# One snapshot of the fifth output product instead of two, and another order of the output products

## The chip, the cores and the metric

The kernel runs on one core of one Trainium2 chip. The metric is the time of one execution in device microseconds, as the median of several runs. Engines are named as the profile names them: PE (TensorE matmul), PEld (TensorE weight load), DVE (VectorE), ACT (ScalarE), POOL (GpSimd), SP (SyncE, which here only issues transfers).

## The reference, cut to what matters

Attention over 8 batches, 8 heads, 576 positions and a head size of 64, then a bilinear feed-forward layer:

```python
rel = pos[:, None] - pos[None, :]
mask_local = (rel >= 0) & (rel < 32)                                   # heads 0 to 3
mask_strided = (rel >= 0) & (pos[None, :] % 32 == pos[:, None] % 32)   # heads 4 to 7
scores = np.where(mask, scale * q @ k.T, -1e9)
attn = softmax(scores) @ v                        # (8, 8, 576, 64)
x = attn.transpose(0, 2, 1, 3).reshape(4608, 512)
out = ((x @ w_a) * (x @ w_b)) @ w_out             # d_ff = 1536, out (4608, 512)
```

Both masks keep so few positions that the kernel works on small groups of them (96 or 72 queries against 128 or 72 keys) and not on the whole square.

## The kernel before

**Tiles and slots.** The 4,608 tokens are nine tiles `t` of 512. A tile has sixteen slots: twelve slots `ffn_ab` (line 581: the products of `x` with a block of `w_a` and of `w_b`, eight matmuls of 512 columns; ACT copies the first, line 598; DVE multiplies it with the second into `pf`, line 601), then four slots of the output product. The attention of batch t+1 runs in the slots of tile t, so that its results `xT` are there for the next tile. The order on every engine is the order of the program: nothing is rescheduled, and each engine works its queue from the front.

**Attention steps.** Each batch has eight steps `S0` to `S7` and eight steps `V0` to `V7`, two for each pair of heads. An `S` step is a group of small matmuls into the PSUM tile `st` (line 384), an exponential by ACT (line 392) and a mask by DVE (line 402). A `V` step is a group of six or eight small matmuls into the PSUM tile `o` (line 485), a logarithm and an exponential by ACT (lines 494 and 495, which make the reciprocal of the row sums) and two multiplications by DVE into `xT` (lines 499 and 501). There is one `st` and, from the second tile on, one `o`, so a `V` step can begin on PE only when the two multiplications of the `V` step before it have read `o`. The dictionary `LATER` gives the slots of these steps; `IN_Y` gives the last three, which lie between products of the output stage.

**Output stage of tiles 2 to 7.** `y_plan` works the product with `w_out` by a scheme of Strassen's kind. Halves of `pf` and sums of halves (`ps`, line 615, by DVE) meet halves of `w_out` and sums of halves (`wf`) in seven products, named "1" to "7". Each is made for two halves of its rows, q = 0 and 1; in `Y_ORDER` "50" is product 5, q = 0. One such half is six matmuls of 256 columns (line 669). Three PSUM tiles collect them, each of exactly one bank, with q = 0 in its first half and q = 1 in its second: X takes products 1, 6, 5 and 3 one after the other on top of each other, Z takes 7 and then 4, Y takes 2. Because X is a running sum, ACT must copy its state out (a "snapshot") before the next product adds to it. `y_post` does that: for 1, 7, 6 and 5 an ACT copy (line 646), for 3 an ACT copy (line 652), for 4 and 2 an addition by DVE (lines 648 and 650), and "+" adds 7's copy to 5's snapshot (DVE, line 644). All are done for both halves together when q = 1 is complete; only product 5 is copied half by half, 128x256 after "50" and 128x256 after "51". A call `take(("y", t, n))` behind the n-th entry of `Y_ORDER` runs the attention step that `IN_Y` has at n. When all is done, two transfers from SP store the tile (line 664), in slots 2 and 3 of the next tile.

**Last tile.** `y_tail` works the same products for tile 8, in `TAIL_ORDER`, with a bank of its own for each half (in the trace `mm` and, for q = 1, `end`; matmuls at line 700). It has no attention beside it and stores each quarter as soon as it is complete: through SP after "+" of 50 and of 51 and after 20, through ACT's queue after 31, and after 21, whose columns are cut in two, once through ACT and once through SP (line 635).

**Pacing of loads.** POOL issues the loads of later batches. Before those of a slot, it copies one element of that slot's result (`pace`, line 908), so that the loads do not run ahead. In the third of the four output slots the element lies in the part of `y` that holds product 5's snapshot.

Of the kernel before, what the change touches and what calls it, by code (L numbers as in the profile page):

```python
# [30 lines left out]
def kernel(  # L31
# [139 lines left out]
    def fast_w(n, gs):  # L171
        a, b = ((wov[:, 0, 1], wov[:, 0, 0]), (wov[:, 1, 1], wf[:, 0]), (wov[:, 1, 1], wov[:, 0, 1]),
                (wov[:, 1, 0], wf[:, 1]))[n]
        nc.vector.tensor_tensor(wf[:, n, gs], a[:, gs], b[:, gs], op=ALU.subtract)
# [349 lines left out]
    def step_X(b, c):  # L524
# [19 lines left out]
                 27.5: "V4", 28: "S6", 28.5: "V5", 29: "S7", 29.5: "V6", 30.5: "V7"}}  # L544
    LATER = {-1: "S0", 0: "S1", 1: "V0", 2: "S2", 3: "V1", 4: "S3", 5: "V2", 6: "S4", 7: "V3", 8: "S5", 9: "V4", 10: "S6",
             11: "V5"}
    IN_Y = {3: "S7", 5: "V6", 11: "V7"}
    FN = {"Tk": step_Tk, "Tq": step_Tq, "S": step_S, "V": step_V, "X": step_X, "W": lambda b, n: fast_w(n, slice(0, 3)),
          "s": S_px, "m": S_m, "L": lead_vl, "Pk": lambda b, c: pair_up("k", c), "Pq": lambda b, c: pair_up("q", c),
          "Z": lambda b, n: zero_qz(0, nc.vector, ((1, 1),)), "D": lambda b, n: step_D(FIRST_D, 0, "k", n)}  # L550
# [8 lines left out]
    def take(pos):  # L559
        for b, names in steps.get(pos, ()):  # L560
            run(b, names)
# [5 lines left out]
    def mm_bank(shape):  # L567
        nm = "tp" if used[0] % 4 == 3 and used[0] >= 0 else "mm"
        used[0] += 1
        return psum4[nm].tile(shape, F32, tag=nm, name="mm")  # L570
# [49 lines left out]
    def products(t):  # L620
        pf, s = pfs[t], pss[t]
        full = lambda e, i: (lambda g, q: pf[:, 2 * g + e, HT * i + q:HT * (i + 1):2])
        summed = lambda n: (lambda g, q: s[:, n, g, q:HT:2])
        wsum = lambda n: (lambda g: wf[:, n, g])
        wfull = lambda e, j: (lambda g: wov[:, e, j, g])
        return {"1": ("X", full(0, 0), wfull(0, 0)), "2": ("Y", full(1, 0), wfull(1, 0)), "3": ("X", summed(3), wfull(1, 1)),
                "4": ("Z", full(1, 1), wsum(3)), "5": ("X", summed(0), wsum(0)), "6": ("X", summed(1), wsum(1)),
                "7": ("Z", summed(2), wsum(2))}
# [8 lines left out]
    def y_bufs():  # L637
        return [fsb.tile([128, 2, d_model], F32, tag="y_sb", name="y_sb", bufs=2) for _ in range(2)]

    def y_post(k, y, q, bank, n=slice(0, HN)):  # L640

        part = lambda i, j: y[i][:, q, HN * j:HN * (j + 1)]
        if k == "+":
            nc.vector.tensor_tensor(part(1, 1), part(1, 1), part(0, 1), op=ALU.add)
        elif k in "1765":
            nc.scalar.copy({"1": part(0, 0), "7": part(0, 1), "6": part(1, 0), "5": part(1, 1)}[k], bank)  # L646
        elif k == "4":
            nc.vector.tensor_tensor(part(1, 0), bank, part(1, 0), op=ALU.add)
        elif k == "2":
            nc.vector.tensor_tensor(y[0][:, q, n], bank, y[0][:, q, n], op=ALU.add)  # L650
        elif k == "3":
            nc.scalar.copy(part(0, 1), bank)

    Y_ORDER = [(x[0], int(x[1])) for x in "10 11 70 71 20 60 61 40 41 50 51 21 30 31".split()]
    TAIL_ORDER = [(x[0], int(x[1])) for x in "10 70 11 71 60 61 40 41 50 51 30 20 31 21".split()]

    def y_plan(t):

        plan, y = products(t), y_bufs()
        bank = {x: mm_bank([128, 2, HN]) for x in "ZXY"}  # L660

        def store_half(i):
            rows = out[TTOK * t:TTOK * (t + 1)].rearrange("(a i s q) c -> a s i (q c)", i=2, s=8, q=2)
            nc.sync.dma_start(out=rows[:, :, i], in_=y[i].rearrange("p q c -> p (q c)"))

        for n, (k, q) in enumerate(Y_ORDER):
            b, lhs, rhs = plan[k]
            for g in range(FG):
                nc.tensor.matmul(bank[b][:, q], lhsT=lhs(g, q), rhs=rhs(g), start=k in "172" and q == 0 and g == 0,  # L669
                                 stop=g == FG - 1, skip_group_check=True)  # L670
                if g == FG - 1:
                    if k == "5":
                        y_post(k, y, q, bank[b][:, q])
                    elif q == 1:
                        y_post(k, y, slice(0, 2), bank[b])
                    if (k, q) == ("5", 1):
                        y_post("+", y, slice(0, 2), None)
                    take(("y", t, n + 1))
                yield y
        do(16 * t + 18, store_half, 0)  # L680
        do(16 * t + 19, store_half, 1)

    def y_tail(t):
# [4 lines left out]
                  "Z": pst.tile([128, 2, 512], F32, tag="st", name="end")[:, 0, :HN]}]  # L688
        for k, q in TAIL_ORDER:
            b, lhs, rhs = plan[k]  # L690
# [25 lines left out]
    def ffn_ys(t, j, mid):  # L716
        if j == 0:
            yst[t] = (y_tail if t == NT - 1 else y_plan)(t)
        for i in range(21):
            y = next(yst[t])  # L720
            if i == 10:
                mid()
        if j == 3:
            for _ in yst[t]:
                pass
        return (y[0][:1, 0, :1], None, y[1][:1, 0, HN:HN + 1], y[1][:1, 0, :1])[j]
# [36 lines left out]
    with tc.manual_schedule(engines={ENG.PE, ENG.SP, ENG.Pool, ENG.DVE, ENG.Activation}):  # L763
# [76 lines left out]
        for b in range(1, B):  # L840
            for pos, names in (STEPS.get(b) or {16 * (b - 1) + x: n for x, n in LATER.items()}).items():
                steps.setdefault(pos, []).append((b, names.split()))
            if b not in STEPS:
                for n, names in IN_Y.items():
                    steps["y", b - 1, n] = [(b, names.split())]
# [3 lines left out]
        def do(i, fn, *args):  # L849
            at.setdefault(i, []).append(lambda: fn(*args))  # L850
# [91 lines left out]
```

## Time and profile before

| | before |
|---|---|
| median of 3 runs | 334.27 us (333.74 to 334.72) |
| profiled execution, its time | 333.48 us |
| profiled execution, its span | 331.7 us |
| PE, PEld busy | 320.4 us (97%), 205.2 us (62%) |
| DVE, ACT, POOL busy | 252.6 (76%), 211.3 (64%), 151.0 us (46%) |
| granted TensorE clock | 1.00 |
| span of one middle tile (93 to 128 us) | 35.0 us |
| output stage in it (116.10 to 127.04 us) | 10.94 us |

A row of the timeline has the start, the duration and the engine of an instruction or of several alike, then line, operation, the tile written and those read, and in brackets how long the engine had been idle and what released it. Matmuls are pipelined: the next starts before the last has drained, so the time that PE gives to a group is read from start to start and not from the durations.

### The profile page before, as it was taken

Reading aid. Unit: us, or ns where it says so; the run is one execution under the profiler, and the core shown is the slowest. Engines: PE = TensorE matmul, PEld = TensorE weight load, DVE = VectorE, ACT = ScalarE, POOL = GpSimd, SP = SyncE. Lnnn points to the kernel's source line nnn. Section 1 sums busy time; section 2 is a strip of 40 time slices with the busy share of each in tenths; the row PEclk is TensorE's granted clock in tenths of the full one; section 3 lists DMA queues with packets and bytes.
Section 4 is the critical chain, followed back from the end, with each engine's and each line's share of the span. In section 5 each row is a group of like instructions: output and inputs, shape, how many; then the busy total and the mean of one; then the engine's idle time right before and its main releaser. Section 6 shows DMA issues by size and latency. Waiting matters only on the chain.

```text
span 331.7 us, 7639 instructions
## 1 busy us (share of the span) xinstructions
PE 320.4 (97%) x2788; PEld 205.2 (62%) x2820; DVE 252.6 (76%) x529; ACT 211.3 (64%) x351; POOL 151.0 (46%) x280
## 2 busy tenths in 40 slices
PE   8999999999999999999999999999999999999994
PEld 6754655455555576557899875567555854574474
DVE  7766978889778997899879977997878655626652
ACT  6764775487788766887577767876777643333341
POOL 8936838699866355654366455543011001100000
PEclk9999999999999999999999999999999999999999
DMA  9999999999998987999889996998023040004004
GB/s 159 152 205 196 204 178 207 147 172 130 131 208 125 86 90 66 118 207 100 76 83 216 102 103 51 195 135 97 0 73 116 2 129 0 0 3 126 0 2 126
DMA packets 98725, 37.50 MB, mean 113 GB/s; under 512 B 76672, under 2 KB 95744, under 8 KB 98688
## 3 DMA queue, kind: packets, MB, share of 16 engines
q0 software_dynamic: 85968, 19.48, 63.5%
q1 hardware_dynamic: 12432, 17.34, 17.8%
q8 instruction: 22, 0.36, 0.5%
q10 hardware_dynamic: 288, 0.20, 0.2%
q14 instruction: 15, 0.12, 0.1%
HBM read 39.51 MB, written 9.44 MB: 148 GB/s over the span
## 4 chain that ended last, share of the span: by engine, by line
PE 87%; DVE 6%; ACT 3%; issue 2%; DMA 1%; SPq 0%; DVEq 0%
PE mm L581 50%; PE mm L669 14%; PE mm L734 6%; PE st L384 4%; PE o L485 4%; DVE xT L501 2%; PE mm L700 2%; PE o L441 1%; DVE pf L601 1%; DMA raw<-in_q_dram 1%; PE end L700 1%; DVE ps L615 1%; PE ab L581 1%; DVE tq L326 1%; ACT xr L495 1%
## 5 line engine op out<-in xcount | busy, mean ns | idle before, releaser
L581 PE MATMUL mm<-xT,wb_sb 128*128 128x512 bf16 (+1 forms) x465 | 109.1, 357 | 0.2
L581 PE MATMUL mm<-xT,wa_sb 128*128 128x512 bf16 (+1 forms) x451 | 107.7, 356 | 1.1
L598 ACT COPY a_sb<-mm 128x512 f32<-128x512 f32 x106 | 62.0, 585 | 45.3 <-PE mm L581 44.6
L908 POOL CAST pace<-pf 1x1 f32<-1x1 bf16 x87 | 24.5, 281 | 122.6 <-DVE pf L601 120.2
L581 PEld LDWEIGHTS <-wb_sb 128*128 128x128 bf16 x480 | 46.3, 98 | 44.0 <-issue 0.2
L601 DVE TENSOR_TENSOR pf<-a_sb,mm 128x512 bf16<-128x512 f32 x84 | 57.0, 678 | 18.2 <-PE mm L581 14.2
L581 PEld LDWEIGHTS <-wa_sb 128*128 128x128 bf16 x480 | 42.7, 98 | 31.2
L392 ACT ACTIVATE p<-st 128x576 bf16<-128x576 f32 (+1 forms) x64 | 41.6, 650 | 7.6 <-PE st L384 7.0
L494 ACT ACTIVATE xr<-o 64x576 f32<-64x576 f32 x48 | 31.1, 647 | 23.8 <-PE o L485 23.5
L495 ACT ACTIVATE xr<-xr 64x576 f32<-64x576 f32 x48 | 32.8, 683 | 1.5
L669 PEld LDWEIGHTS <-ps 128*128 128x128 bf16 x288 | 27.5, 98 | 6.8 <-issue 3.8
L499 DVE TENSOR_TENSOR xT<-o,xr 64x288 bf16<-64x288 f32 x48 | 21.6, 449 | 13.3 <-ACT xr L495 12.7
L669 PE MATMUL mm<-wf,ps 128*128 128x256 bf16 x216 | 28.3, 272 | 2.8 <-ACT y_sb L646 2.8
L646 ACT COPY y_sb<-mm 128x512 f32<-128x512 f32 (+1 forms) x34 | 16.5, 485 | 20.6 <-PE mm L669 17.3
L501 DVE TENSOR_TENSOR xT<-o,xr 64x288 bf16<-64x288 f32 x48 | 21.6, 449 | 9.9 <-ACT xr L495 9.4
L734 PE MATMUL mm<-wo_sb,pf 128*128 128x512 bf16 x93 | 22.9, 379 | 0.1
L669 PEld LDWEIGHTS <-pf 128*128 128x128 bf16 x216 | 20.6, 98 | 2.7 <-issue 0.2
L242 POOL DMA_DIRECT2D vs<-in_v_dram x24 | 19.6, 818 | 5.0 <-ACT p L392 2.4
L669 PE MATMUL mm<-wo_sb,pf 128*128 128x256 bf16 x144 | 18.7, 272 | 0.1
L211 POOL DMA_DIRECT2D ql<-in_q_dram x24 | 16.0, 665 | 5.6 <-DMA wo_sb<-in_moe_w_out_dram 4.5
L211 POOL DMA_DIRECT2D kl<-in_k_dram x24 | 16.0, 666 | 5.0 <-issue 3.2
L615 DVE TENSOR_TENSOR ps<-pf 128x512 bf16<-128x512 bf16 (+1 forms) x48 | 17.7, 380 | 0.5
(152 smaller groups left out, 468.6 us busy)
## 6 DMA issues: line engine op xcount, KB each, us to landing
out_dram<-y_sb SPq DMA_DIRECT2D x12, 512.0 KB, 4.8
out_dram<-y_sb SPq DMA_DIRECT2D x11, 256.0 KB, 3.0
vl<-in_v_dram POOLq DMA_DIRECT2D x6, 384.0 KB, 6.4
kl<-in_k_dram POOLq DMA_DIRECT2D x24, 72.0 KB, 3.2
ql<-in_q_dram POOLq DMA_DIRECT2D x24, 72.0 KB, 3.7
vs<-in_v_dram POOLq DMA_DIRECT2D x24, 72.0 KB, 3.9
wo_sb<-in_moe_w_out_dram POOLq DMA_DIRECT2D x4, 384.0 KB, 9.6
natk<-in_k_dram POOLq DMA_DIRECT2D x20, 72.0 KB, 3.5
```

The costliest lines, as they stand in the source:

```text
L211: nc.gpsimd.dma_start(out=t[32 * h:32 * h + 32], in_=src[b, h].rearrange("(i y) d -> y i d", y=32))
L392: nc.scalar.activation(p[:M, :, :W], st[:M, :, :W], ACT.Exp, scale=scale)
L494: nc.scalar.activation(r, sums, ACT.Ln)
L495: nc.scalar.activation(r, r, ACT.Exp, scale=-1.0)
L499: nc.vector.tensor_mul(dst[:, W * half:W * (half + 1)], o[:64, j, :W], r[:, j])
L501: nc.vector.tensor_mul(dst.rearrange("d (p r) -> d p r", r=RS)[:, :, G * half:G * (half + 1)], o[:64, j, :W].rearrange("d (g p) -> d p g", ...
L581: nc.tensor.matmul(ps_[:, c0:c0 + n], lhsT=w[:, kk, 128 * f:128 * (f + 1)], rhs=xT[:, kk, x0:x0 + n], start=(kk == first and c0 == 0), sto ...
L598: nc.scalar.copy(a_sb, ab[0])
L601: nc.vector.tensor_mul(pf[:, f, :].rearrange("p (i a s) -> p a i s", i=2, s=16), halves(a_sb), halves(ab[1]))
L669: nc.tensor.matmul(bank[b][:, q], lhsT=lhs(g, q), rhs=rhs(g), start=k in "172" and q == 0 and g == 0, stop=g == FG - 1, skip_group_check=True)
L734: nc.tensor.matmul(ybank[j], lhsT=pf[:, f, 128 * j:128 * (j + 1)], rhs=wo_sb[:, f], start=(f == 0), stop=(f == FD - 1))
L908: nc.gpsimd.tensor_copy(pace, done)
```

## The change

The snapshot of product 5 becomes one copy of 128x512 after "51", as it is for the other products. Product 2 is no longer split: in `Y_ORDER` its first half moves from between 71 and 60 to behind 51, so that 20 and 21 both lie between 51 and 30. `IN_Y` moves with it: S7 from behind the first half of product 7 to ahead of it (behind 11), V6 from behind 20 to behind 61, and V7 stays eleventh, which is now between 20 and 21 where it was between 51 and 21. In the last tile 31 moves ahead of 20, and the stores that hang on 31 and on 20 with them.

```diff
-    IN_Y = {3: "S7", 5: "V6", 11: "V7"}
+    IN_Y = {2: "S7", 6: "V6", 11: "V7"}
...
-    Y_ORDER = [(x[0], int(x[1])) for x in "10 11 70 71 20 60 61 40 41 50 51 21 30 31".split()]
-    TAIL_ORDER = [(x[0], int(x[1])) for x in "10 70 11 71 60 61 40 41 50 51 30 20 31 21".split()]
+    Y_ORDER = [(x[0], int(x[1])) for x in "10 11 70 71 60 61 40 41 50 51 20 21 30 31".split()]
+    TAIL_ORDER = [(x[0], int(x[1])) for x in "10 70 11 71 60 61 40 41 50 51 30 31 20 21".split()]
...
                 if g == FG - 1:
-                    if k == "5":
-                        y_post(k, y, q, bank[b][:, q])
-                    elif q == 1:
+                    if q == 1:
                         y_post(k, y, slice(0, 2), bank[b])
-                    if (k, q) == ("5", 1):
-                        y_post("+", y, slice(0, 2), None)
+                        if k == "5":
+                            y_post("+", y, slice(0, 2), None)
                     take(("y", t, n + 1))
```

The sequences of an output stage, with the attention steps in their places:

| | order on PE |
|---|---|
| before | 10 11 70 S7 71 20 V6 60 61 40 41 50 51 V7 21 30 31 |
| after | 10 11 S7 70 71 60 61 V6 40 41 50 51 20 V7 21 30 31 |

The number of matmuls does not change. ACT has one instruction less in each of six tiles. In DVE's queue "+" moves ahead of one transposition (line 331).

## The prediction

> **What bounds the kernel now.** I read the page first, then PE's waits, then the timeline of one output stage, last a table of all six.
>
> ```profile
> PE 320.4 (97%) x2788; PEld 205.2 (62%) x2820; DVE 252.6 (76%) x529; ACT 211.3 (64%) x351; POOL 151.0 (46%) x280
> L581 PE MATMUL mm<-xT,wb_sb 128*128 128x512 bf16 (+1 forms) x465 | 109.1, 357 | 0.2
> ```
>
> PE bounds it: 97% busy, and the large matmuls of line 581 lost 0.2 us to idling. So only time that PE loses inside the output stages can be won. PE's waits name it:
>
> ```profile
> PE mm L669 <- ACT y_sb L646: 2.8, 6, 0.5
> PE o L485 <- DVE xT L501: 0.6, 3, 0.2
> ```
>
> Six times (once for each of tiles 2 to 7) a product waits for a snapshot; three times a V step waits for DVE. The timeline of tile 2's stage shows the places:
>
> ```profile
> 118.95 0.91 DVE L501 TENSOR_TENSOR xT<-o,xr 64x288 bf16<-64x288 f32 x2
> 118.99 0.82 PE L669 MATMUL mm<-wo_sb,pf 128*128 128x256 bf16 x6
> 120.00 0.42 PE L485 MATMUL o<-p,vs 72*128 72x72 bf16 x8 [0.20 <-DVE xT L501]
> 121.57 1.47 PE L669 MATMUL mm<-wf,pf 128*128 128x256 bf16 x12
> 122.88 0.82 PE L669 MATMUL mm<-wf,ps 128*128 128x256 bf16 x6
> 123.73 0.37 ACT L646 COPY y_sb<-mm 128x256 f32<-128x256 f32 x1 [1.30 <-PE mm L669]
> 124.16 0.81 PE L669 MATMUL mm<-wf,ps 128*128 128x256 bf16 x6 [0.46 <-ACT y_sb L646]
> ```
>
> The row at 122.88 is 50, the copy at 123.73 its half snapshot, the row at 124.16 is 51. They use different halves of bank X, yet 51 starts 0.06 us after the copy's end (124.10). Twelve matmuls (40 and 41) took 122.88 - 121.57 = 1.31 us, 0.109 each, so 51 could have started at 122.88 + 0.66 = 123.54: the loss is 0.62 us, more than the 0.46 of the row, which counts from the modelled end. In the same way 20 (118.99) would have let V6 in at 119.65; V6 came at 120.00, 0.14 us after V5's multiplications, which end at 119.86: 0.35 us lost.
>
> All six stages, from the start of 10 to the first matmul behind 31:
>
> ```profile
> 116.10:127.04 10.94, 10.29 (x115) 8.94 (x112) 9.02 (x19) 7.14 (x12) 6.56 (x13) 1.00 0.76 87
> 151.10:162.03 10.93, 10.28 (x114) 8.94 (x111) 9.01 (x19) 7.14 (x12) 6.57 (x13) 1.00 0.76 85
> 186.59:197.23 10.64, 10.18 (x108) 8.91 (x108) 8.75 (x18) 7.09 (x12) 6.55 (x13) 1.00 0.78 87
> 221.29:232.23 10.94, 10.28 (x114) 8.93 (x111) 9.02 (x19) 7.14 (x12) 4.44 (x9) 1.00 0.69 85
> 256.30:266.88 10.58, 10.12 (x113) 9.00 (x111) 6.58 (x15) 7.14 (x12) 0.25 (x2) 1.00 0.01 2
> 287.60:297.39 9.79, 9.33 (x86) 8.23 (x84) 4.23 (x8) 2.50 (x5) 0.37 (x1) 1.00 0.01 2
> ```
>
> First comes the length. Without a wait a stage takes 84 x 0.1093 = 9.18 us, and in the first five 0.77 more for S7, V6 and V7 (0.26, 0.25, 0.26 from start to start): 9.95. The excess is 0.99, 0.98, 0.69, 0.99, 0.63 and 0.61: 4.89 us in all, 6 x 0.62 = 3.7 of it before 51, the rest before V6 (0.36, 0.35, 0.07, 0.36, 0). The clock was 1.00 in all of them.
>
> **The change, step by step.** Times from here on count from the start of 10 in tile 2, with no wait: 10 at 0, 11 at 0.66, S7 1.32, 70 1.58, 71 2.23, 60 2.89, 61 3.55, V6 4.20, 40 4.45, 41 5.11, 50 5.76, 51 6.42, 20 7.07, V7 7.73, 21 7.98, 30 8.64, 31 9.30, end 9.95. Each must find what it needs; the times of ACT and DVE come from rows of the same timeline, moved with the PE row that releases them.
>
> *One snapshot of product 5.* 51 follows 50 with nothing to wait for: -0.62 us in six stages, -3.7. The wait goes to 30, the next to add to X. A whole copy takes 0.58 (rows of other products) and starts about 0.31 after the last matmul's start (6.97): 7.28 to 7.87. With 0.06 to release, 30 could go at 7.93 and is due at 8.64: 0.71 spare, 0.45 in tile 7, which has no V7. The cover is 20, V7 and 21 (1.57 us); without it the stage would lose about 0.9. ACT works 0.58 instead of 2 x 0.37 us, which PE does not feel.
>
> *Where page and row differ.* The rows at 122.88 to 124.16 show the half copy causing PE's pause. The Trainium skill, Perfetto Trace Analysis, section "Optimizing Scalar/DVE Operations", says that where Scalar or Vector are not saturated but cause bubbles elsewhere, breaking up their instructions may let work finish sooner. ACT is at 64%, so by that rule the halves should stay; merging would cost 0.58 - 0.37 = 0.21 us in six stages, +1.3 us, if 30 stood right behind the copy, and the whole change would come to +0.3 and 334.6 us. I go by the rows.
>
> *V6 behind 61.* V5's multiplications end at 3.76, release at 3.90; V6 is due at 4.20: -1.14 us in all. Its p was masked long before (step S6). Next is V7, which waits for V6's chain, and that now starts with an ACT queue holding 6's snapshot ahead of it: snapshot 4.41 to 5.00, logarithm and exponential (0.65, 0.68) to 6.38, multiplications 6.41 to 7.30 (DVE is free from 5.44). V7 may go at 7.45 and is due at 7.73: 0.28 spare, the smallest margin here.
>
> *S7 ahead of 70.* Its bank `st` was read before the stage began. ACT takes 1's snapshot, S7's exponential and 7's snapshot in the order of before: nothing.
>
> *60 earlier.* It needs 1's snapshot (ended at 2.18, due 2.89) and the last `ps` rows, which DVE finished at 2.92. Those are for its fifth and sixth matmuls, at 3.33: spare 0.4.
>
> *DVE, SP, POOL.* "+" runs at about 8.6 and then one transposition, so V7's multiplications start near 9.9 and end by 10.9; the next tile reads them after S0 and six large matmuls, at 11.46: nothing. The moved steps issue no transfer; SP's order in tiles 2 to 7 stays. The third `pace` now waits for "+" and not for 50's copy, 9.4 instead of 8.1; behind it in POOL's queue stand the loads kl and ql, which landed by 128.7 and are read from 137.8 on: hidden. If they were late, DVE's transpositions would be, and then S0.
>
> *Last tile.*
>
> ```profile
> 324.89 0.37 ACT L646 COPY y_sb<-end 128x256 f32<-128x256 f32 x1 [0.28 <-PE end L700]
> 326.00 0.82 PE L700 MATMUL end<-wo_sb,ps 128*128 128x256 bf16 x6
> 327.19 0.63 DVE L650 TENSOR_TENSOR y_sb<-mm,y_sb 128x128 f32<-128x128 f32 x2 [0.57 <-PE mm L700]
> out_dram<-y_sb SPq DMA_DIRECT2D x3, 256.0 KB, 2.9
> ```
>
> 31 moves from 326.00 to 325.35 and needs 51's copy, over at 325.26 plus 0.06: it just fits. Its 128 KB go out 0.65 us earlier, the 256 KB of 20 by 0.65 later (issue 327.3), and DVE's additions for 21 start 0.1 later, behind that of 20. With 2.9 us to landing the 256 KB arrive at 330.2, about when the last store landed (issued 327.9, 2.6 us). Bounds: -0.2 (ACT's last store freed of the one ahead of it) to +0.4 us (the engines empty 0.4 later). I take +0.1, nearer to the landing row.
>
> *Sum.* -3.74 - 1.14 + 0.1 = -4.8 us. For small losses at margins under 0.4 us I give back 0.1: -4.7. The profiled execution took 333.48 us (span 331.7, the rest lies around it); 333.48 - 4.7 = 328.8; the median lay 0.79 above, so 329.6 us.
>
> **The rivals.**
> *V7 takes over V6's wait.* Margin 0.28 us; if ACT or DVE come 0.3 to 0.6 later than I reckon, five stages lose 0.05 to 0.3. With V6's 1.14 gone entirely: 334.27 - 3.7 = 330.6, range 330.3 to 331.5. For it: V6 did just that. Against it: DVE idled 0.32 us before V6's multiplications, so it isn't late there. 0.22.
> *The faster stage outruns something behind it.* Tile 4's S4 started at 176.04, its last transfer landed at 175.62. DVE is busy for 30.6 of tile 3's 35 us. A loss of 0.3 us in each of five tiles and the V6 part gone: 332.1. Against it: DVE still idles 0.9, 0.8 and 0.4 us early in tile 3's first slots (before rows of line 499), where it catches up. 0.05.
> *It doesn't remove the wait.* If 51 were held by something else of X, only V6's part would come: 333.1, at the edge of no change, and no change if one margin fails as well. Against it: the release 0.06 us after the copy, six times. 0.05.
> *Slower: 5's snapshot comes late.* If ACT gets to it after V7's logarithm and exponential (8.19 to 9.55), it ends at 10.14, and 30 goes at 10.2 instead of 8.64: 1.56 lost in five stages, 7.8 against 4.9 won, 337.2 us. It costs from a start of the copy after 8.0, and turns the sum from 8.85 on. For it: ACT's queue is in order, and such a pair takes 1.36 us. Against it: the copy is queued ahead of V7's pair, and ACT is free from 6.4. 0.06.
>
> **How the numbers follow.** The forecast has 0.62 (328.8 to 330.3: the tail's bounds and the spread of the runs, 0.5 each way); with V7's wait 0.84. The range 328.6 to 331.6 takes in both and leaves some 0.16 out. A measurement can tell about 0.3%, 1.0 us, from no change. Faster: 0.62 + 0.22 + 0.05 = 0.89; same 0.05; slower 0.06.
>
> **What would show it.** Right: PE's waits have no row of line 669 for ACT, 51 starts 0.66 us after 50, the stages take 9.95 and 9.18 us, ACT has six instructions fewer with copies of 0.58 us. Half right: a row "PE o" for DVE xT at V7. Wrong: 30 released by an ACT copy, the first matmuls of the next tile idle, or a stage above 10.6 us.

## The result, and the profile after

The changed kernel took 329.66 us (median of 4 runs, 329.22 to 330.64), beside 334.19 us for the kernel before (333.74 to 334.72): a ratio of 0.9868, 95% interval 0.984 to 0.9896. The prediction was 329.6 us, between 328.6 and 331.6. Some executions, of the kernel before too, ran at a mean granted clock of 0.980 to 0.990 and took some 3 to 6 us longer than the others of their kernel: one of the six of e2 below, three of the six of e9, one of the six of e12.

Line 669 is the output stage in both kernels; below `y_plan` the changed kernel's lines are lower by two. First the busy time and the number of instructions of each engine, then the whole list of PE's waits:

```profile
PE 322.3 (98%) x2820; PEld 206.2 (63%) x2820; DVE 251.6 (76%) x529; ACT 210.2 (64%) x345; POOL 151.4 (46%) x280
```

```profile
PE misc L154 <- PEq L924: 0.9, 1, 0.9
PE o L441 <- DMA tk<-in_v_dram: 0.6, 1, 0.6
PE tp L286 <- ACT shared L798: 0.5, 1, 0.5
PE o L441 <- DMA vl<-in_v_dram: 0.3, 1, 0.3
```

There is no row of line 669 and none of line 485 left; these four belong to the first 20 us, before anything that was changed. ACT has 345 instructions where it had 351. The timeline of PE in tile 2's stage (it starts at 118.09) runs from group to group:

```profile
119.66 2.79 PE L669 MATMUL mm<-wf,ps 128*128 128x256 bf16 x24
122.28 0.43 PE L485 MATMUL o<-p,vs 72*128 72x72 bf16 x8
122.55 1.48 PE L669 MATMUL mm<-wf,pf 128*128 128x256 bf16 x12
123.86 1.47 PE L669 MATMUL mm<-wf,ps 128*128 128x256 bf16 x12
125.17 0.82 PE L669 MATMUL mm<-wo_sb,pf 128*128 128x256 bf16 x6
125.82 0.42 PE L485 MATMUL o<-p,vs 72*128 72x72 bf16 x8
```

The rows are 70 to 61 in one piece, V6, 40 and 41, 50 and 51, 20, and V7. V6 comes 2.62 us after 70 began, which is 24 matmuls at 0.109; 51 follows 50 within one row. No row has a bracket for idle time. In the same stage ACT makes product 5's whole copy, and DVE the two multiplications of V6:

```profile
125.37 0.59 ACT L646 COPY y_sb<-mm 128x512 f32<-128x512 f32 x1 [0.86 <-PE mm L669]
124.54 0.92 DVE L501 TENSOR_TENSOR xT<-o,xr 64x288 bf16<-64x288 f32 x2 [1.01 <-ACT xr L495]
```

The six stages, by stretch (length first, then busy time and number for PE, PEld, DVE, ACT and POOL, then the granted clock and two figures of the DMA engines):

```profile
118.09:128.05 9.96, 9.96 (x114) 9.02 (x111) 8.75 (x19) 6.88 (x11) 4.32 (x9) 1.00 0.68 77
152.12:162.08 9.96, 9.96 (x114) 9.00 (x111) 8.75 (x19) 6.88 (x11) 4.33 (x9) 1.00 0.69 77
186.64:196.60 9.96, 9.96 (x109) 9.00 (x109) 8.50 (x18) 6.83 (x11) 4.32 (x9) 1.00 0.68 76
220.66:230.62 9.96, 9.96 (x114) 9.00 (x111) 8.75 (x19) 6.89 (x11) 4.46 (x9) 1.00 0.72 78
254.69:264.65 9.96, 9.96 (x113) 9.00 (x111) 6.62 (x15) 6.89 (x11) 0.26 (x2) 1.00 0.01 2
285.37:294.54 9.17, 9.17 (x85) 8.22 (x84) 4.34 (x8) 2.34 (x4) 0.37 (x1) 1.00 0.01 2
```

PE is busy for the whole of each. They add up to 58.97 us where they added up to 63.82: 4.85 us. (The end of tile 6's stage in the kernel before, 266.88, is worked out at 0.109 us per matmul: the first matmul behind it has no record in the trace.) The rest of the way from the first stage to the last tile's products, with no output stage in it, took 138.2 us in both kernels.

This profiled execution took 330.64 us, the longest of the four, and its first stage began at 118.09 us where it was 116.10: at 18.3 to 21.7 us the granted clock was 0.50 (more on that at the end). So the difference of the two spans, 2.8 us, is less than what the stages gave.

### The profile page after: what moved, and what is told of

Its sections match the earlier page's. It is cut to its first block, busy times and chain, and to the rows that moved or that the text cites. A ratio compares the mean times of both kernels' runs of the same rounds, so it can differ in the third digit from the quotient of the medians.

```text
span 328.9 us, 7658 instructions
## 1 busy us (share of the span) xinstructions
PE 322.3 (98%) x2820; PEld 206.2 (63%) x2820; DVE 251.6 (76%) x529; ACT 210.2 (64%) x345; POOL 151.4 (46%) x280
## 3 DMA queue, kind: packets, MB, share of 16 engines
q1 hardware_dynamic: 12432, 17.34, 17.7%
## 4 chain that ended last, share of the span: by engine, by line
PE 93%; POOL 2%; DMA 2%; DVE 1%; ACT 0%; issue 0%; POOLq 0%
PE mm L581 55%; PE mm L669 17%; PE mm L732 6%; PE st L384 4%; PE o L485 4%; DMA tk<-in_v_dram 2%; PE mm L698 2%; PE ab L581 1%; POOL shared L196 1%; PE end L698 1%; PE o L441 1%; POOL vl L224 1%; PE tp L510 1%; PE tp L286 0%; PE tp L295 0%
## 5 line engine op out<-in xcount | busy, mean ns | idle before, releaser
L581 PE MATMUL mm<-xT,wa_sb 128*128 128x512 bf16 (+1 forms) x472 | 110.3, 357 | 0.0
L646 ACT COPY y_sb<-mm 128x512 f32<-128x512 f32 (+1 forms) x28 | 15.6, 556 | 18.5 <-PE mm L669 13.0
L669 PE MATMUL mm<-wf,ps 128*128 128x256 bf16 x216 | 25.6, 273 | 0.0
```

The costliest lines, as they stand in the source:

```text
L581: nc.tensor.matmul(ps_[:, c0:c0 + n], lhsT=w[:, kk, 128 * f:128 * (f + 1)], rhs=xT[:, kk, x0:x0 + n], start=(kk == first and c0 == 0), sto ...
```

## The experiments

Their stage lengths are read as above; the lengths of tiles 2 to 6 stand ahead of that of tile 7. In five runs (e1, e3, e5, e6, e7) the third `pace` reads an element of product 6's part of `y`: in those kernels product 5's last copy comes only after that pace, which would otherwise read `y` before it is written. A control (e8) has that edit alone.

### e1: the whole copy, in the old order

```diff
 # the changed kernel with the orders and IN_Y of before
-    ... y[1][:1, 0, HN:HN + 1], y[1][:1, 0, :1])[j]
+    ... y[1][:1, 0, :1], y[1][:1, 0, :1])[j]
```

> The order of the kernel before, with product 5 copied whole after 51 (V6 still between 20 and 60, V7 and 21 between 51 and 30). So that the copy is made before it is read, the third pace reads an element of product 6's part of y. Theory (each half of bank X is held while ACT reads the other): the 0.62 us before 51 go in six stages, 3.7 us; V6's waits of 0.36, 0.35, 0.07, 0.36 stay; in tile 7, with 21 alone as cover, 30 waits 0.19 us. Stages near 10.33, 10.32, 10.02, 10.32, 9.95, 9.37; time 334.2 - 3.5 = 330.7 us. Rival (merging moves the wait to 30, which waits as long as 51 did): stages as before, 334.2 us.

Measured: 10.31, 10.31, 10.02, 10.31, 9.96 and 9.35 us, 60.26 in all, 3.56 us less than before; 330.0 us, ratio 0.9882 (0.9867 to 0.9897). Of PE's waits in the stages one row is left:

```profile
PE o L485 <- DVE xT L501: 0.6, 3, 0.2
```

It is the row of before: V6's waits. The wait before 51 is gone and hardly any of it moved to 30 (9.35 where 9.17 needs no wait: 0.18 us, in tile 7 alone). The copy alone is worth three quarters of the change.

### e2: the new order, with the copy in halves

```diff
 # the kernel before with the orders and IN_Y of the changed one
```

> The order of the changed kernel with product 5 still copied in halves. Theory: 51 waits 0.62 us in six stages as before; V6 behind 61 finds the o bank free, -1.14 us. Stages near 10.57 in the first five and 9.79 in tile 7; time 334.2 - 1.1 = 333.1 us. Rival (the order alone is what won the time, because 50 meets an ACT that is free earlier): no wait before 51 and 329.7 us.

Measured: 10.58 us in each of the first five stages and 9.79 in tile 7, 62.69 in all, 1.13 us less than before; 332.95 us, ratio 0.9959 (0.9945 to 0.9973).

```profile
PE mm L669 <- ACT y_sb L646: 2.8, 6, 0.5
```

Now it is V6's row that is gone, and this one is as it was. The two parts add up: 3.56 + 1.13 = 4.69 us, and the 0.18 that e1 loses at 30 in tile 7 makes 4.87, against 4.85 for the whole.

### e3: V6 behind 61, but 20 left in its old place

```diff
-    IN_Y = {3: "S7", 5: "V6", 11: "V7"}
+    IN_Y = {3: "S7", 7: "V6", 11: "V7"}
 # orders as before, one copy of product 5, third pace as in e1
```

> Whole copy of product 5, V6 behind 61, but 20 left between 71 and 60; the third pace reads product 6's part. This takes one product (0.66 us) out from between V6 and V7. Theory: V7 needs 3.23 us from V6's start (0.46 to the logarithm or later behind 6's snapshot, 0.65 + 0.68 on ACT, 0.9 on DVE, 0.15 release) and now has 2.87, so it waits 0.36 us in five stages, a row of PE waits at V7 of some 1 us in all (counted from modelled ends); tile 7 loses 0.19 at 30. Time 329.7 + 1.8 + 0.2 = 331.7 us. Rival (the 0.28 us of margin is underestimated, V7 never waits): 329.9 us.

Measured: 10.31, 10.31, 10.30, 10.31, 10.30 and 9.35 us; 331.03 us, ratio 0.9911 (0.9895 to 0.9927). PE's waits, and the place of one in its timeline:

```profile
PE o L485 <- DVE xT L501: 0.9, 5, 0.2
```

```profile
122.81 1.47 PE L669 MATMUL mm<-wf,ps 128*128 128x256 bf16 x12
124.45 0.43 PE L485 MATMUL o<-p,vs 72*128 72x72 bf16 x8 [0.17 <-DVE xT L501]
```

51's last matmul began at 124.01 and V7 could have followed at 124.12; it came at 124.45, 0.33 us late, in this stage and alike in the other four. This is the rival "V7 takes over V6's wait", made true by taking one product out from between them. So the move of product 2 does more than cover 30: it gives V6 its place without making V7 wait.

### e5 and e7: nothing but V7 between 51 and 30

```diff
-    Y_ORDER = ... "10 11 70 71 60 61 40 41 50 51 20 21 30 31"
+    Y_ORDER = ... "10 11 70 71 20 21 60 61 40 41 50 51 30 31"
-    IN_Y = {2: "S7", 6: "V6", 11: "V7"}
+    IN_Y = {2: "S7", 6: "V6", 12: "V7"}
 # third pace as in e1; e5 with the copy whole, e7 with the copy in halves
```

> The changed kernel with both halves of product 2 moved away from between 51 and 30 (10 11 S7 70 71 20 21 V6 (behind 20 and 21's first place, with its o bank free) 60 61 40 41 50 51 V7 30 31): only V7, 0.26 us, lies between 51 and 30; the third pace reads product 6's part. Theory: the whole copy ends 0.55 + 0.31 + 0.58 + 0.06 = 1.50 us after 51's first matmul and 30 is due at 0.92, so 30 waits 0.58 us in five stages and 0.84 in tile 7: 3.7 us more than the changed kernel, 333.4 us. Rival (the wait before 51 was not one of bank X, so 30 will not wait either): 329.7 us.

> The order of the run without cover, with product 5 copied in halves. Theory: 51 waits 0.62 us in six stages, then 30 waits for the second half's copy, 0.37 us in five stages and 0.63 in tile 7: 6.2 us more than the changed kernel, 335.9 us, 2.5 us more than with the whole copy. Rival (the page's rule: smaller copies let the next product start sooner): faster than the whole copy in the same order, by 6 x 0.21 = 1.3 us.

Measured: with the whole copy 10.53 us in five stages and 10.00 in tile 7, 332.53 us, ratio 0.9957 (0.9938 to 0.9975); with halves 10.94 and 10.41, 335.63 us, ratio 1.0043 (1.0024 to 1.0062). PE's timeline in the first stage of e5, then of e7:

```profile
122.85 1.47 PE L669 MATMUL mm<-wf,ps 128*128 128x256 bf16 x12
124.16 0.42 PE L485 MATMUL o<-p,vs 72*128 72x72 bf16 x8
125.00 1.47 PE L669 MATMUL mm<-wo_sb,ps 128*128 128x256 bf16 x12 [0.41 <-ACT y_sb L646]
```

```profile
125.99 0.81 PE L669 MATMUL mm<-wf,ps 128*128 128x256 bf16 x6 [0.46 <-ACT y_sb L646]
126.65 0.42 PE L485 MATMUL o<-p,vs 72*128 72x72 bf16 x8
127.27 1.47 PE L669 MATMUL mm<-wo_sb,ps 128*128 128x256 bf16 x12 [0.20 <-ACT y_sb L646]
```

With one copy, 30 waits once; with two, 51 waits and then 30 as well. Even where the whole copy has almost no cover, it costs 0.57 us per stage against 0.98. The Trainium skill (Perfetto Trace Analysis, "Optimizing Scalar/DVE Operations") says that breaking up instructions of Scalar or Vector may let work finish sooner where these engines are not saturated and cause idle time elsewhere. Here it is the other way round by 2.5 us of stage time: both halves lie in one PSUM tile of one bank, and each copy makes PE wait. The last tile shows halves that make nothing wait, in the timelines of PE and ACT in the kernel before:

```profile
323.38 0.82 PE L700 MATMUL mm<-wf,ps 128*128 128x256 bf16 x6
324.03 0.82 PE L700 MATMUL end<-wf,ps 128*128 128x256 bf16 x6
324.23 0.37 ACT L646 COPY y_sb<-mm 128x256 f32<-128x256 f32 x1 [1.59 <-PE mm L700]
```

These are 50 and 51 in `y_tail`, each with a tile and a bank of its own, and the copy of 50. It ran from 324.23 to 324.60, and 51 had started 0.65 us after 50, with no wait.

### e6: the slower rival made true

```diff
                 if g == FG - 1:
-                    if q == 1:
+                    if q == 1 and k != "5":
                         y_post(k, y, slice(0, 2), bank[b])
-                        if k == "5":
-                            y_post("+", y, slice(0, 2), None)
                     take(("y", t, n + 1))
+                    if (k, q) == ("2", 0):
+                        y_post("5", y, slice(0, 2), bank["X"])
+                        y_post("+", y, slice(0, 2), None)
 # third pace as in e1
```

> The changed kernel with product 5's copy and the addition behind it queued after V7, so that ACT makes V7's logarithm and exponential first; the third pace reads product 6's part. This is the prediction's slower rival made true. Theory: the copy starts 9.56 us after 10's start and 30 goes at 10.2 instead of 8.64: 1.56 us in each of five stages, none in tile 7, 7.8 in all, 337.5 us. If ACT's place in the queue does not matter because 30 has slack: 329.7 us.

Measured: 11.53, 11.53, 11.51, 11.52, 11.53 and 9.17 us; 337.11 us, ratio 1.0076 (1.0048 to 1.0105). ACT and PE in the first stage, which starts at 116.80:

```profile
125.00 0.65 ACT L494 ACTIVATE xr<-o 64x576 f32<-64x576 f32 x1 [1.79 <-PE o L485]
125.68 0.68 ACT L495 ACTIVATE xr<-xr 64x576 f32<-64x576 f32 x1
126.39 0.59 ACT L646 COPY y_sb<-mm 128x512 f32<-128x512 f32 x1
```

```profile
127.02 1.14 PE L669 MATMUL mm<-wo_sb,ps 128*128 128x256 bf16 x9 [1.40 <-ACT y_sb L646]
```

Product 5 was complete long before: ACT idled 1.79 us ahead of V7's pair and could have copied it then. Behind the pair the copy ends at 126.98, and 30 goes at 127.02, 10.22 after the stage's start. The same copy, two places later in one queue, turns 1.3% won into 0.8% lost.

### e4 and e8 to e12: the last tile's order, and the pace

```diff
-    TAIL_ORDER = ... "10 70 11 71 60 61 40 41 50 51 30 31 20 21"
+    TAIL_ORDER = ... "10 70 11 71 60 61 40 41 50 51 30 20 31 21"
 # e4, e10, e11: the changed kernel with this; e9, e12: the changed kernel; e8: its third pace as in e1
```

> The changed kernel with the last tile's order of before (30 20 31 21). Theory: the tail's edit moves the end by -0.2 to +0.4 us, best +0.1, so this takes 329.6 us; from the first matmul of the last tile's products to the end of the span as long as in the kernel before, 13.64 us. Rival (the earlier 128 KB store is worth something): 0.3 us or more slower than the changed kernel, 330.0 us.

> The changed kernel unchanged, beside the run with the old tail on the same chip. If the tail's edit is worth nothing (tails of 13.64 to 13.74 us in six profiles with either order), both medians lie within 0.3 us of each other, near 329.3. If the old tail is better, as 328.84 against 329.66 in two separate calls would have it, this one is slower by 0.5 us or more.

> The changed kernel with the last tile's order of before, again, beside the changed kernel on the same chip: the same time within 0.3 us if the tail's edit is worth nothing, 0.5 us or more faster if the old tail is better.

> The changed kernel with the last tile's order of before, a third time, ahead of the changed kernel on the same chip. If the two differ only by executions with a lowered clock, the executions at a clock of 0.997 and over lie within 0.4 us of the changed kernel's, and lowered clocks turn up in both. If the old tail is better, it is 0.5 us or more ahead at full clock.

> The changed kernel a third time: at a clock of 0.997 and over between 328.6 and 329.9 us as before, within 0.4 us of the old tail on the same chip, if the tail's edit is worth nothing; 0.5 us or more behind if it costs.

> The changed kernel with the third pace reading an element of product 6's part of y instead of product 5's, as in four other runs. Theory: the loads behind it go out earlier by a microsecond and nothing waits for them: stages of 9.96 and 9.18 us, 329.7 us. Rival (the pace sets something): a stage differs by over 0.1 us.

Measured, old tail: 328.84 (ratio 0.9842, 0.9828 to 0.9857), 328.77 (0.9837, 0.982 to 0.9853) and 329.22 us (0.9835, 0.9787 to 0.9883). New tail on the same chips: none beside the first; 331.01 (0.9899, 0.9864 to 0.9934) beside the second; 328.99 us (0.9845, 0.9793 to 0.9898) beside the third. The 331.01 looked like a cost of the new tail and was not: beside the three long executions named with the result, the other three took 328.66, 329.21 and 330.23 us. In the third pair the new tail is ahead by 0.2. From the first product of the last tile to the end of the span the profiles show 13.60 to 13.78 us with the old order (six, with the kernel before, e1 and e3) and 13.65 to 13.72 with the new one (eight, three of them of the changed kernel). The edit of the last tile is worth nothing that these runs can tell.

The pace alone (e8): 329.83 us in one run, stages of 9.96 and 9.17 us; it sets nothing, so the five runs with that edit can be read as they stand.

## Why the prediction was right, step by step

*51 waits for bank X's other half:* confirmed. With the copy whole (e1) the wait goes, with halves (e2) it stays, with banks apart (the last tile) there is none. Predicted 0.62 us in each of six stages; e2's stages are longer than the changed kernel's by 0.62. The program sets this wait; whether the chip would need it was not tried. X is one tile as well as one bank, and the last tile parts both, so the runs do not show which of the two the wait goes by.

*30 takes the wait but has cover:* the copy in the changed kernel ran from 7.28 to 7.87 after the stage's start (125.37 to 125.96), as worked out. Cover taken away costs 0.57 and 0.83 us (e5), where e5's expectation had 0.58 and 0.84.

*V6 behind 61:* 1.13 us (e2) against 1.14 worked out. *V7's margin* was taken as 0.28 us and was smaller: the multiplications of V6 ended at 125.46, 7.37 after the start and not 7.30, which with 0.15 for the release leaves 0.21. It held in all five stages. One product less and it breaks (e3).

*"+", `pace`, DVE's order:* "+" started 8.60 after the start (8.6 predicted), V7's multiplications 9.82 to 10.70 (9.9 to 10.9), and the next tile's matmuls waited for neither.

*The last tile:* +0.1 us, taken with bounds of -0.2 and +0.4, is within what the profiles scatter (0.1).

*The sum:* 4.88 us of stage time predicted, 4.85 measured. The 0.1 given back for small margins was not needed; with the 0.1 for the tail it accounts for 0.2 us of caution, less than two executions of the same kernel differ by. That the median came within 0.06 us of the forecast is luck: the same kernel's median was 331.01 us in e9 and 328.99 us in e12. The stage times test the mechanism.

*The price of merging by the page's rule:* the prediction put it at +1.3 us if 30 stood right behind the copy. That counts a wait at 30 alone and leaves out that halves make 51 wait too. With only V7 between 51 and 30, merging won 2.5 us of stage time (e7 against e5). The forecast did not use this price.

*The rivals:* V7's wait was real but one product away, the late snapshot real but two places away in ACT's queue. The point from which that late copy costs more than the change wins was put at 8.85; 4.8 us over five stages is 0.96, past 8.0, so 8.96; in e6 the copy started at 9.59, beyond both. Nothing behind the stages was outrun: the stretches between them took 138.2 us in every profile, with stages that add up to between 58.97 and 66.8 us.

## What to carry to other kernels

Here a PSUM tile of one bank behaved as one object: while one half was being copied out, the matmul that writes the other half waited, until 0.06 us after the copy's end. So a copy in two halves made two waits where a whole copy made one (e7 and e5). Ask of such a copy not how long it is but what stands between it and the next write to its bank, on PE and in the copying engine's own queue, and put independent products there. Read such waits from start to start: six waits listed at 0.46 us were 0.62 us each of PE's time.

## What was not expected

In the profiled execution of the changed kernel PE ran at half its clock for one stretch, early and in code that is the same in both kernels (length, busy times as above, then the clock):

```profile
14.90:18.30 3.40, 2.81 (x79) 2.37 (x76) 3.03 (x8) 1.78 (x3) 2.43 (x4) 1.00 1.41 196
18.30:21.70 3.40, 3.40 (x31) 1.92 (x30) 1.78 (x5) 1.71 (x3) 1.29 (x3) 0.50 1.31 204
21.70:25.10 3.40, 3.40 (x24) 1.68 (x23) 0.74 (x2) 1.94 (x4) 0.95 (x2) 1.00 1.25 206
```

e7's profile shows the same from 17.7 to 21.2 us; the other profiles have no such stretch there. It cost 3.40 x 0.5 = 1.7 us, most of the 2.0 by which the first stage began late. The Trainium skill (TensorE: Matmul & The Clock Gate, Part 1) has a window of 3.4 us and a half clock after an idle one; length and clock agree, the idle window does not: PE was busy for 2.81 of the 3.40 us before, and for 2.99 in the kernel before, which kept its clock. Nor does a low share of busy time do it by itself: in e10 PE was busy for 2.66 of the 3.41 us from 12.22 on, and in the 3.41 us behind these the clock was still 1.00. What sets it off here stays open. For the reader of such runs it means that the spans of two profiles can differ by 2 us from their first 26 us alone, and that the stretch in question must be compared by itself.
